# Sparse attention followed by an ELU MoE layer on one Trainium2 core: attention rewritten in residue-class and 96-query blocks, with one table set and a hand-fixed order

## The chip, the cores and the metric

The kernel runs on one core of one Trainium2 chip. The metric is the device time of one execution in microseconds (us), taken over several runs. A ratio is over fast runs alone; it can differ by up to 0.005 from the quotient of the medians that are quoted beside it. Every experiment was timed beside the kernel before on the same chip; experiments of different rounds are therefore compared by their ratios to the kernel before.

The engines are named as in the profile: PE is TensorE's matmuls, PEld its weight loads, ACT is ScalarE, DVE is VectorE, POOL is GpSimd, SP is the queue that stores the output. PSUM is the memory that TensorE's results lie in until another engine has read them. In the chain of waits, "issue" is time in which an engine waited for nothing that the profile shows.

## The reference

Eight batches, eight heads, 576 tokens, head width 64. Heads 0 to 3 look at the last 32 tokens; heads 4 to 7 look at all earlier tokens with the same remainder modulo 32. The attention output is the input of two dense layers with an ELU between them.

```python
scores = q @ k.T / sqrt(64)
rel = pos[:, None] - pos[None, :]
mask_local   = (rel >= 0) & (rel < 32)
mask_strided = (rel >= 0) & (pos[None, :] % 32 == pos[:, None] % 32)
attn = softmax(where(mask, scores, -1e9))        # local for heads 0-3, strided for 4-7
x = (attn @ v)  as [8*576, 512]
h = x @ w_in                                     # 512 -> 2048
g = where(h > 0, h, exp(min(h, 0)) - 1)
out = g @ w_out                                  # 2048 -> 512
```

## The kernel before

Queries and keys are cut into five blocks of 128. A strided head computes every pair of blocks on or below the diagonal and multiplies by a mask; a local head computes the diagonal block and its neighbour. Both heads of a pair are transposed together. The denominators come from a V widened by 64 columns of ones, and are inverted as Exp(-Ln(x)).

```python
for s in range(NQ):                       # blocks of 128 keys
    nq_all = NQ - s if is_str else min(2, NQ - s)
    ...
        nc.tensor.matmul(sc_ps[:, :Nq], lhsT=kT[pb:pb + D, s, :], rhs=qT[...])        # L191
        nc.scalar.activation(exp_sb[:, :Nq], sc_ps[:, :Nq], ACT.Exp, scale=scale)     # L201
        nc.vector.tensor_mul(msk_sb[:, :Nq], exp_sb[:, :Nq], mask_cat[...])           # L207
        nc.tensor.matmul(acc_ps[...], lhsT=v_sb[:, s, p, :], rhs=msk_sb[...])         # L220
nc.scalar.activation(ln_sb[D:2*D, :], acc_ps[D:2*D, ...], ACT.Ln)                     # L235
nc.scalar.activation(recip_sb[D:2*D, :], ln_sb[D:2*D, :], ACT.Exp, scale=-1.0)        # L242
nc.vector.tensor_mul(xT[...], acc_ps[0:D, ...], recip_sb[D:2*D, :S])                  # L247
# after each batch: one chunk of 512 tokens of the MoE
for m in range(16):                       # first layer: 4 matmuls of 512 columns (L269),
    ...                                   # Exp (L276), min/subtract (L279), max (L283)
for kk in range(4):                       # second layer: 16 matmuls (L289), copy (L296), store
    ...
```

The order of each engine's instructions is chosen by the framework's scheduler, which mixes a batch's attention with the MoE of an earlier chunk.

The softmax here doesn't subtract the row's maximum and nothing guards it: scores larger than these inputs give would overflow.

## Time and profile before

| | before |
|---|---|
| median of 4 runs | 684.73 us (678.51 to 685.74) |
| TensorE busy | 503.7 us, 74% |
| ScalarE busy | 480.6 us, 71% |
| MoE matmuls at full pace (estimate: 1152 x 0.216) | 249 us |
| table loads on ScalarE | 129 x 1.283 = 165.5 us |
| mean granted TensorE clock | 0.861 |

The first fence is from the page: busy time, share of the span and instructions of each engine, then the busy tenths in 40 slices for TensorE with the clock granted to it, then the chain of waits by engine.

```profile
PE 503.7 (74%) x2304; PEld 210.1 (31%) x2304; DVE 347.3 (51%) x907; ACT 480.6 (71%) x789; POOL 259.5 (38%) x404
...
PE   0356677779577886989678866878776977679996
...
PEclk9999996899888686569877896589678876999999
...
PE 45%; ACT 28%; issue 17%; DVE 4%; DMA 4%; POOL 1%; ACTq 0%; DVEq 0%; POOLq 0%
```

No engine is full. The clock falls in many slices in the middle, where TensorE's work has gaps.

The groups by form (line, engine, operation, shapes and count, then busy us and mean ns of one, then idle us before it):

```profile
L269 PE MATMUL hps<-xT,w_in_sb 128*128 128x512 bf16 x576 | 199.6, 446 | 9.7 <-DVE xT L247 7.5 <-DVE g_sb L283 1.8
L235 ACT ACT_TABLE_LOAD x64 | 82.1, 1283 | 1.1
L201 ACT ACT_TABLE_LOAD x35 | 44.9, 1283 | 1.4 <-PEq L313 0.8
```

The loads stand before Ln (L235) and before whichever Exp comes next: each switch between the two functions loads a table; 19 and 11 more stand before L242 and L276, 129 in all. In the timeline of ScalarE (start, duration, instruction) the load is wedged between the last score and the logarithm that the denominators wait for, and the next Exp pays again:

```profile
32.11 1.28 ACT L235 ACT_TABLE_LOAD   x1
33.41 0.70 ACT L235 ACTIVATE ln_sb<-acc_ps 64x640 f32<-64x640 f32 x1
34.13 1.28 ACT L201 ACT_TABLE_LOAD   x1
35.42 0.38 ACT L201 ACTIVATE exp_sb<-sc_ps 128x256 bf16<-128x256 f32 x1
```

TensorE waits for ScalarE in the scores, as the waits say (engine and line, whom it waited for, us in total, times, longest):

```profile
PE sc_ps L191 <- ACT exp_sb L201: 115.0, 57, 3.7
PE tp_ps L162 <- DMA qh<-in_q_dram: 26.4, 1, 26.4
```

What a gap costs beyond itself is in the windows (stretch, its length, TensorE busy and matmuls, granted clock, DMA share, GB/s). A sparse stretch is followed by one at half the clock:

```profile
176.00:180.00 4.00, 0.87 (x5) 1.00 0.90 58
180.00:184.00 4.00, 4.00 (x15) 0.59 0.64 40
184.00:188.00 4.00, 1.82 (x8) 0.50 0.00 0
```

The Trainium skill ("TensorE: Matmul & The Clock Gate", Part 1) says that TensorE's clock is halved after about 3.4 us of idleness and restored after about as much work. The pace in this trace fits the two levels: in a dense stretch sixteen MoE matmuls take 3.62 us, (3.62 - 0.38) / 15 = 0.216 us from start to start; at a granted clock of 0.5 four take 1.89 us (at 431.13), (1.89 - 0.63) / 3 = 0.42 us.

### The profile page before, as it was taken

How to read it: one execution, taken by the hardware profiler on the slowest of the kernel's cores; microseconds unless marked ns; L12 is line 12 of the kernel's file. 1: busy time of each engine (PE TensorE's matmuls, PEld its weight loads, DVE VectorE, ACT ScalarE, POOL GpSimd, SP SyncE). 2: the span in 40 equal slices, each digit the busy share in tenths (PEclk: the TensorE clock that was granted, in tenths of full speed). 3: DMA queues.
4: the chain of work that ended last, by engine and by line, in shares of the span. 5: the costliest groups of instructions: out<-in, count | busy, mean ns of one | idle time of the engine just before them, and what ended most of it. 6: DMA issues, size and time to landing. Idle time of an engine off the chain costs nothing.

```text
span 680.3 us, 7667 instructions
## 1 busy us (share of the span) xinstructions
PE 503.7 (74%) x2304; PEld 210.1 (31%) x2304; DVE 347.3 (51%) x907; ACT 480.6 (71%) x789; POOL 259.5 (38%) x404
## 2 busy tenths in 40 slices
PE   0356677779577886989678866878776977679996
PEld 0122232224233332323233322333322433234442
DVE  3144355664456444565556544563555635646570
ACT  0287798974888478784988687884879578974341
POOL 6498456560444415343444433352444410000000
PEclk9999996899888686569877896589678876999999
DMA  8988446461444414345344533344444510001101
GB/s 159 127 57 54 26 27 39 28 39 63 27 27 27 55 38 28 22 25 89 26 28 26 58 48 23 20 31 77 28 26 27 57 39 2 1 16 48 47 15 62
DMA packets 124552, 28.29 MB, mean 42 GB/s; under 512 B 117344, under 2 KB 119392, under 8 KB 124512
## 3 DMA queue, kind: packets, MB, share of 16 engines
q0 software_dynamic: 119328, 18.37, 36.7%
q1 hardware_dynamic: 5184, 9.44, 3.7%
q8 instruction: 18, 0.29, 0.2%
q14 instruction: 22, 0.18, 0.1%
HBM read 36.70 MB, written 9.44 MB: 68 GB/s over the span
## 4 chain that ended last, share of the span: by engine, by line
PE 45%; ACT 28%; issue 17%; DVE 4%; DMA 4%; POOL 1%; ACTq 0%; DVEq 0%; POOLq 0%
PE ops L289 15%; PE hps L269 14%; PE sc_ps L191 8%; ACT exp_sb L201 7%; PE acc_ps L220 6%; ACT ln_sb L235 6%; ACT L235 5%; ACT recip_sb L242 4%; ACT e_sb L276 3%; PE tp_ps L162 3%; DMA kh<-in_k_dram 2%; DVE g_sb L283 2%; DMA w_in_sb<-in_moe_w_in_dram 2%; ACT L276 2%; DVE e_sb L279 1%
## 5 line engine op out<-in xcount | busy, mean ns | idle before, releaser
L269 PE MATMUL hps<-xT,w_in_sb 128*128 128x512 bf16 x576 | 199.6, 446 | 9.7 <-DVE xT L247 7.5
L191 PE MATMUL sc_ps<-qT,kT 64*128 64x256 bf16 (+2 forms) x352 | 98.5, 332 | 120.3 <-ACT exp_sb L201 115.0
L201 ACT ACTIVATE exp_sb<-sc_ps 128x256 bf16<-128x256 f32 (+2 forms) x352 | 129.8, 403 | 67.8 <-PE sc_ps L191 63.0
L289 PE MATMUL ops<-w_out_sb,g_sb 128*128 128x512 bf16 x576 | 158.0, 402 | 10.6 <-ACT o_sb L296 6.4
L143 POOL DMA_DIRECT2D vh<-in_v_dram x64 | 52.5, 820 | 196.0 <-PE acc_ps L220 118.3
L276 ACT ACTIVATE e_sb<-hps 128x512 f32<-128x512 f32 x144 | 84.8, 602 | 26.2 <-PE hps L269 25.4
L283 DVE TENSOR_TENSOR g_sb<-e_sb,hps 128x512 bf16<-128x512 bf16 x144 | 97.4, 682 | 2.0
L269 PEld LDWEIGHTS <-w_in_sb 128*128 128x128 bf16 x576 | 53.9, 106 | 139.8 <-issue 108.0
L207 DVE TENSOR_TENSOR msk_sb<-exp_sb,mask_str 128x512 bf16<-128x512 bf16 (+1 forms) x192 | 56.5, 322 | 74.5 <-ACT exp_sb L201 72.2
L207 DVE TENSOR_TENSOR msk_sb<-exp_sb,mask_local 128x256 bf16<-128x256 bf16 (+1 forms) x160 | 41.1, 277 | 99.9 <-ACT exp_sb L201 97.4
L220 PE MATMUL acc_ps<-msk_sb,vh 128*128 128x128 bf16 (+3 forms) x480 | 90.0, 320 | 0.0
L143 POOL DMA_DIRECT2D qh<-in_q_dram x64 | 53.8, 841 | 90.0 <-PE tp_ps L162 71.2
L296 ACT COPY o_sb<-ops 128x512 f32<-128x512 f32 x36 | 21.1, 587 | 91.2 <-PE ops L289 69.8
L289 PEld LDWEIGHTS <-g_sb 128*128 128x128 bf16 x576 | 56.9, 101 | 89.7 <-issue 27.7
L235 ACT ACT_TABLE_LOAD x64 | 82.1, 1283 | 1.1
L247 DVE TENSOR_TENSOR xT<-acc_ps,recip_sb 64x576 bf16<-64x576 f32 x64 | 48.0, 750 | 65.0 <-ACT recip_sb L242 64.0
L279 DVE TENSOR_SCALAR e_sb<-e_sb 128x512 bf16<-128x512 f32 x144 | 61.6, 443 | 30.9 <-ACT e_sb L276 30.6
L191 PEld LDWEIGHTS <-kT 64*128 64x128 bf16 x352 | 27.3, 99 | 147.6 <-issue 128.5
L220 PEld LDWEIGHTS <-vh 128*128 128x128 bf16 x480 | 50.5, 123 | 39.8 <-issue 25.8
L143 POOL DMA_DIRECT2D kh<-in_k_dram x64 | 56.1, 876 | 3.6 <-DMA w_in_sb<-in_moe_w_in_dram 3.6
L235 ACT ACTIVATE ln_sb<-acc_ps 64x640 f32<-64x640 f32 x64 | 44.8, 699 | 6.9 <-PE acc_ps L220 6.2
L242 ACT ACTIVATE recip_sb<-ln_sb 64x640 bf16<-64x640 f32 x64 | 46.9, 733 | 1.3
(38 smaller groups left out, 347.1 us busy)
## 6 DMA issues: line engine op xcount, KB each, us to landing
out_dram<-o_sb SPq DMA_DIRECT2D x36, 256.0 KB, 2.0
qh<-in_q_dram POOLq DMA_DIRECT2D x64, 64.0 KB, 2.7
kh<-in_k_dram POOLq DMA_DIRECT2D x64, 64.0 KB, 2.7
vh<-in_v_dram POOLq DMA_DIRECT2D x64, 64.0 KB, 2.7
w_in_sb<-in_moe_w_in_dram POOLq DMA_DIRECT2D x1, 2048.0 KB, 12.8
w_out_sb<-in_moe_w_out_dram POOLq DMA_DIRECT2D x1, 2048.0 KB, 19.9
qh<-in_q_dram POOLq DMA_DIRECT2D x64, 8.0 KB, 2.1
kh<-in_k_dram POOLq DMA_DIRECT2D x64, 8.0 KB, 2.2
```

What stands on the lines that cost most here:

```text
L143: nc.gpsimd.dma_start(out=t_sb[:, 0:NQ - 1, hi, :D], in_=src[b, h0 + hi, 0:(NQ - 1) * 128, :].rearrange("(slab p) d -> p slab d", p=128),)
L191: nc.tensor.matmul(sc_ps[:, :Nq], lhsT=kT[pb:pb + D, s, :], rhs=qT[pb:pb + D, s0:s0 + nq, :].rearrange("p a b -> p (a b)"), start=True, st ...
L201: nc.scalar.activation(exp_sb[:, :Nq], sc_ps[:, :Nq], ACT.Exp, scale=scale,)
L207: nc.vector.tensor_mul(msk_sb[:, :Nq], exp_sb[:, :Nq], mask_cat[:, chunk0:chunk0 + nq, :].rearrange("p a b -> p (a b)"),)
L220: nc.tensor.matmul(acc_ps[:, t:t + ntt, :].rearrange("p a b -> p (a b)"), lhsT=v_sb[:, s, p, :], rhs=msk_sb[:, tt * 128:(tt + ntt) * 128], ...
L235: nc.scalar.activation(ln_sb[D:2 * D, :], acc_ps[D:2 * D, :, :].rearrange("p a b -> p (a b)"), ACT.Ln,)
L242: nc.scalar.activation(recip_sb[D:2 * D, :], ln_sb[D:2 * D, :], ACT.Exp, scale=-1.0,)
L269: nc.tensor.matmul(hps, lhsT=w_in_sb[:, c, m * 128:(m + 1) * 128], rhs=xblk[:, c, :], start=(c == 0), stop=(c == KC - 1),)
L276: nc.scalar.activation(e_sb, hps, ACT.Exp)
L279: nc.vector.tensor_scalar(e1_sb, e_sb, scalar1=1.0, scalar2=1.0, op0=ALU.min, op1=ALU.subtract,)
L283: nc.vector.tensor_tensor(g_sb[:, m, :], e1_sb, hps, op=ALU.max)
L289: nc.tensor.matmul(ops, lhsT=g_sb[:, m, kk * 128:(kk + 1) * 128], rhs=w_out_sb[:, m, :], start=(m == 0), stop=(m == MC - 1),)
```

## The change

Its intent is to make attention small and to hide it under the MoE. Strided heads are split by the remainder of the token modulo 8: each class has 72 tokens, so a head needs eight blocks of 72 x 72 in place of fifteen of 128 x 128. Local heads use six blocks of 96 queries against 128 keys. Exp and Ln share one table set. The load order puts batch 0's attention ahead of the weights. The instruction order is fixed by hand: one piece of the next batch's attention, four first-layer matmuls, four second-layer matmuls, and so on.

```diff
+    ctx.enter_context(tc.manual_schedule())
+    nc.scalar.preload_act_table_set("natural_log_exp_and_others")
+    p_a = ...("ps_a", bufs=2, PSUM)      # transposes, outputs and sums share this
...
+    def load_str(src, b, name):          # strided heads: runs of 8 tokens, one DMA for 4 heads
+        nc.gpsimd.dma_start(out=t, in_=src[b, HG:2*HG].rearrange("h (p s) d -> p h (s d)", s=NS))
...
+    def piece_T(P):                      # transpose q, then k; one shared buffer each
+        ...  nc.tensor.transpose(ps[:, o:o+RS], src[...], identity[...])
+             nc.vector.tensor_copy(dst, ps)
+    def piece_S(P, u):                   # half of a pair: scores of both halves of the array, Exp, mask
+        nc.tensor.matmul(sc[:, z, i*n:(i+1)*n], lhsT=P.kT[pr, k0:k0+128], rhs=P.qT[pr, o:o+n], ...)
+        nc.scalar.activation(e[0:R], sc[0:R, :, 0:W], ACT.Exp, scale=scale)
+    def piece_O(P, u, pm):               # o_ps and s_ps: both shared buffers
+        ...
+        nc.scalar.activation(ln, s_ps, ACT.Ln)
+        nc.scalar.activation(rc, ln, ACT.Exp, scale=-1.0)
+        if P.str:
+            dst = xs.rearrange("c (p u sp z) -> c u z sp p", u=2, sp=2, z=2)[:, u]
+            nc.vector.tensor_mul(dst, o_ps.rearrange(pat, ...), rc.rearrange(pat, ...))   # L275
+        else:
+            nc.vector.tensor_mul(xs[:, u*W:(u+1)*W], o_ps, rc)                            # L278
...
+    def run_piece(p):
+        old = list(pend); pend.clear()
+        if u < 0: piece_T(...)
+        else:     pend.append(... piece_S(...))
+        for a in old: piece_O(*a)
...
+    for nb in range(NCH):
+        for m in range(MC):
+            run_piece(pieces[done])      # while there are any
+            l1(nb, m)                    # 4 matmuls, Exp, 2 VectorE operations
+            if nb > 0: l2(nb - 1, m)     # 4 matmuls
```

A pair of heads is three pieces: T (transposes), then the two halves. In the order, the outputs of an older half come behind the new piece: T is followed by the outputs of the previous pair's second half, and the second half by those of the first. There are 96 pieces: 14 run alone, 82 are interleaved, and 62 MoE steps are left.

## The prediction

> **What bounds the kernel now.** The span is 680 us and no engine is full: the busy table gives TensorE 504 us (74%), ScalarE 481 (71%), VectorE 347, GpSimd 260. The chain of waits is shared: TensorE 45%, ScalarE 28%, "issue" 17%. TensorE and ScalarE hold each other up in attention. The groups by form show why ScalarE is long: 129 table loads of 1283 ns (165 us) because Ln and Exp use different tables; 352 score exponentials (138 us); Ln and Exp of the denominators over 64x640 (92 us); the MoE needs only 106 us. TensorE's needed work is less than its busy time: in a dense stretch of the timeline, 16 MoE matmuls take 3.62 us, 0.216 us each start to start, so 1152 of them are 249 us. The windows show a granted clock of 1.0 when TensorE is dense (600-680 us), and 0.5 for several us after sparse stretches (184-188, 220-224 us); mean 0.861. At the start the first transpose waits 26.4 us, because both weights are queued ahead of q.
>
> **What changes, costed.**
> - ScalarE: one table set for Ln and Exp. The Trainium skill ("ScalarE: Activation LUTs", Table sets: the hidden batching unit) says one set holds both and gives 1283 ns a load; the trace agrees on the load. -165 us. By the trace's 0.83 ns per element plus about 0.17 us, each of 64 half-pairs costs 0.65 (Exp 576) + 0.41 + 0.41 (Ln, Exp 288) us: 94 us in place of 230. ScalarE falls to about 200 us.
> - VectorE: two copies at 0.45, two mask products at 0.45 and two normalisations at 0.45 us a pair: 87 us, plus 159 of MoE: about 246 us.
> - TensorE: 1472 small matmuls (448 transposes, 448 scores, 576 values and sums) in place of 1152. The trace's dense 128-column transposes start 0.057 us apart; at 0.06 us, 46 a pair are 2.8 us. Seven changes of tile shape a pair cost about 0.1 us each (the timeline shows that much beyond the streaming time; the skill's "TensorEngine Tiling", Key Properties, says that a change of mode drains the array). Tiny matmuls add about 110 us to 249: TensorE about 360 us, now the bound.
> - DMA: strided heads load in 1 KB runs; packets fall from 119 thousand to about 70 thousand. Not the bound, except at the start.
>
> **Critical path, in four parts.**
> 1. Batch 0's attention plus two pieces, alone: about 13 us until q, k and the identity are there, then 14 pieces at 2.6 us, latency-bound because transposes, outputs and sums share two PSUM buffers: about 50 us.
> 2. 82 interleaved steps. A pair's three steps: 3 x 1.73 (eight MoE matmuls) + 2.8 + 0.7 + about 0.9 of waiting in the transpose step for VectorE to empty those two buffers = 9.5 us, 3.2 a step: 262 us, less 14 for chunk 0, which has no second layer.
> 3. 62 steps of MoE alone at 1.73: 107 us.
> 4. Last second layer 14 us, copy and store 3 us; some clock dips, 8 us.
>
> Sum: 430 us; range 398 to 480. Ratio about 0.63.
>
> **Right if:** at most two table loads; TensorE above 85% busy with the clock near 1.0 after 60 us; ScalarE about 30% of the chain or less; first MoE matmul at 45-60 us; attention ends near 300 us; last 62 steps at 1.73 us.
>
> **Wrong if:** table loads remain (about 550 us); small matmuls cost 0.1 us or more, since 64-column weight loads and shape changes do not overlap (+50 us); in-order queues make TensorE wait each step for ScalarE or VectorE, and the clock drops to half again (+50 us or more); or batch 0's local heads, still in 128-byte packets, come late.
>
> Chances: faster by over 2% 0.98, within 2% 0.01, slower 0.01.

## The result, and the profile after

The kernel after takes 423.29 us (median of 4 runs, 420.37 to 423.34) against 684.73: the ratio is 0.6187, 95% interval 0.6153 to 0.6222. The same parts of the page, after:

```profile
PE 345.6 (82%) x2584; PEld 171.2 (41%) x2624; DVE 271.7 (64%) x501; ACT 196.7 (47%) x373; POOL 88.9 (21%) x120
...
PE   0256776678888878888887888888999999999996
...
PEclk9999988989988998998999889899999999999999
...
PE 61%; DVE 15%; DMA 9%; ACT 6%; issue 4%; POOL 4%; POOLq 0%; ACTq 0%
```

ScalarE has left the chain (28% to 6%); TensorE and VectorE hold it. The groups:

```profile
L318 PE MATMUL hps<-xT,w_in_sb 128*128 128x512 bf16 x542 | 152.4, 403 | 5.5 <-issue 5.2
...
L275 DVE TENSOR_TENSOR xT<-o_ps,rc 128x288 bf16<-128x288 f32 x32 | 46.0, 1437 | 20.0 <-ACT rc L269 20.0
...
L278 DVE TENSOR_TENSOR xT<-o_ps,rc 128x288 bf16<-128x288 f32 x32 | 14.6, 458 | 19.0 <-ACT rc L269 19.0
...
L61 ACT ACT_TABLE_LOAD x1 | 1.3, 1283 | 0.8 <-PEq L388 0.8
```

One table load is left. The two normalisations have the same size, 288 elements on 128 partitions, but the strided heads' one (L275) takes three times the other's time.

The stages, from the first and last instructions in the timeline, beside those of the prediction:

| stage | predicted us | measured us |
|---|---|---|
| batch 0 and two pieces, until the first MoE matmul's weights are loaded | 50 | 43.9 |
| 82 interleaved steps | 262 - 14 = 248 | 252.4 (43.9 to 296.3) |
| 62 steps of MoE alone | 107 | 106.4 (1.72 each) |
| last second layer, copy, store | 17, and 8 for the clock anywhere | 18.9 |

The windows of the last two stages (columns: stretch, length, busy us and count of PE, PEld, DVE, ACT and POOL, granted clock, DMA share, GB/s) show where the kernel is good and where not:

```profile
96.00:296.00 200.00, 169.94 (x1470) 84.47 (x1491) 144.22 (x261) 107.09 (x211) 38.77 (x49) 0.94 0.47 56
296.00:403.00 107.00, 106.37 (x493) 48.54 (x502) 69.64 (x126) 46.22 (x79) 0.00 (x0) 1.00 0.10 38
```

In the interleaved stage TensorE stands still 15% of the time and does not have its full clock. Why is in its timeline, over one pair of strided heads (in brackets the idle time before an instruction, and what ended it):

```profile
151.03 0.30 PE L217 MATMUL sc<-qT_130,kT_127 64*128 64x72 bf16 x8
151.27 1.04 PE L318 MATMUL hps<-xT,w_in_sb 128*128 128x512 bf16 x4
...
155.45 0.42 PE L185 MATMUL tp<-identity,qs 72*128 72x72 bf16 x8
156.62 0.42 PE L185 MATMUL tp<-identity,ks 72*128 72x72 bf16 x8 [0.76 <-DVE xT L275]
157.97 0.45 PE L240 MATMUL s_ps<-pm,ones 72*64 72x288 bf16 x2 [0.92 <-DVE qT_131 L196]
...
159.11 1.49 PE L318 MATMUL hps<-xT,w_in_sb 128*128 128x512 bf16 x3 [0.33 <-issue]
```

The two half pieces take 2.07 and 2.35 us with their eight MoE matmuls. The T piece, from 155.45 to the next scores at 161.85, takes 6.40. It is one of the longest: from 85 us on the T pieces take 3.98 to 6.67 us, 4.96 on average (22 of them), and the long ones are those that run into half clock. The clock record has 11 stretches at half clock between 59 and 274 us, of 3.41 us each. The transposes of k need the buffer that the previous outputs still hold, and wait for their normalisation; the sums need the buffer of q, and wait for its copy; then the MoE matmuls behind them start 0.43 us apart in place of 0.216 - half the clock. VectorE's timeline of the same stretch shows what was in front of that copy: the slow strided normalisation and the two ELU operations of the previous step.

```profile
155.14 1.44 DVE L275 TENSOR_TENSOR xT<-o_ps,rc 128x288 bf16<-128x288 f32 x1 [0.32 <-ACT rc L269]
156.20 0.62 DVE L325 TENSOR_SCALAR he_1943<-he 128x512 bf16<-128x512 f32 x1
156.86 0.69 DVE L327 TENSOR_TENSOR g<-he_1943,hps 128x512 bf16<-128x512 bf16 x1
157.46 0.45 DVE L196 COPY qT_131<-tp 128x576 bf16<-128x576 bf16 x1
```

So the total was predicted to 2%, but the middle stage holds a stall that is larger than the one predicted, and something else must be smaller. The experiments take this apart, and measure what the table set, the interleaving and the fixed order are worth. No run changes the block sizes or the load order alone.

### The profile page after: what moved, and what is told of

Its sections match the earlier page's. It is cut to its first block, busy times and chain, and to the rows that moved or that the text cites. A ratio compares the mean times of both kernels' runs of the same rounds, so it can differ in the third digit from the quotient of the medians.

```text
span 421.6 us, 6645 instructions
## 1 busy us (share of the span) xinstructions
PE 345.6 (82%) x2584; PEld 171.2 (41%) x2624; DVE 271.7 (64%) x501; ACT 196.7 (47%) x373; POOL 88.9 (21%) x120
## 4 chain that ended last, share of the span: by engine, by line
PE 61%; DVE 15%; DMA 9%; ACT 6%; issue 4%; POOL 4%; POOLq 0%; ACTq 0%
PE hps L318 28%; PE ops L339 27%; DVE xT L275 4%; DVE g L327 4%; DMA ks<-in_k_dram 3%; DMA qs<-in_q_dram 3%; PE sc L217 3%; ACT he L323 2%; DMA vs<-in_v_dram 2%; PE o_ps L261 1%; ACT e L221 1%; ACT rc L269 1%; PE o_ps L249 1%; PE s_ps L256 1%; ACT osb L344 1%
## 5 line engine op out<-in xcount | busy, mean ns | idle before, releaser
L318 PE MATMUL hps<-xT,w_in_sb 128*128 128x512 bf16 x542 | 152.4, 403 | 5.5 <-issue 5.2
L339 PE MATMUL ops<-w_out_sb,g 128*128 128x512 bf16 x570 | 151.0, 392 | 0.4
L323 ACT ACTIVATE he<-hps 128x512 f32<-128x512 f32 x144 | 85.8, 596 | 87.3 <-PE hps L318 84.4
L339 PEld LDWEIGHTS <-g 128*128 128x128 bf16 x576 | 58.0, 101 | 72.6 <-issue 8.2
L221 ACT ACTIVATE e<-sc 72x576 bf16<-72x576 f32 (+1 forms) x64 | 41.4, 648 | 42.6 <-PE sc L217 41.3
L275 DVE TENSOR_TENSOR xT<-o_ps,rc 128x288 bf16<-128x288 f32 x32 | 46.0, 1437 | 20.0 <-ACT rc L269 20.0
L267 ACT ACTIVATE ln<-s_ps 128x288 f32<-128x288 f32 x64 | 26.1, 407 | 68.9 <-PE s_ps L240 39.1
L75 POOL DMA_DIRECT2D ql<-in_q_dram x32 | 23.6, 747 | 38.4 <-PE tp L192 27.2
L269 ACT ACTIVATE rc<-ln 128x288 f32<-128x288 f32 x64 | 28.3, 443 | 2.0
L75 POOL DMA_DIRECT2D kl<-in_k_dram x32 | 23.8, 755 | 16.5 <-DMA qs<-in_q_dram 6.2
L278 DVE TENSOR_TENSOR xT<-o_ps,rc 128x288 bf16<-128x288 f32 x32 | 14.6, 458 | 19.0 <-ACT rc L269 19.0
L185 PE MATMUL tp<-identity,qs 72*128 72x72 bf16 x128 | 7.7, 210 | 14.5 <-POOL identity L112 13.9
```

The source lines that it names most:

```text
L75: nc.gpsimd.dma_start(out=t[:, h // 2, :, h % 2, :], in_=src[b, h].rearrange("(t p) d -> p t d", p=LQ))
L185: nc.tensor.transpose(ps[:, o:o + RS], src[:, P.g0 + x, 2 * sp * D:2 * (sp + 1) * D], identity[0:RS, 0:RS])
L221: nc.scalar.activation(e[0:R], sc[0:R, :, 0:W], ACT.Exp, scale=scale)
L267: nc.scalar.activation(ln, s_ps, ACT.Ln)
L269: nc.scalar.activation(rc, ln, ACT.Exp, scale=-1.0)
L275: nc.vector.tensor_mul(dst, o_ps.rearrange(pat, z=2, sp=2), rc.rearrange(pat, z=2, sp=2))
```

## The experiments

Twelve kernels ran. Ratios are to the kernel before; the change itself has 0.6187.

### One table set in the kernel before, nothing else

```diff
     nc = tc.nc
+    nc.scalar.preload_act_table_set("natural_log_exp_and_others")
```

> The kernel before plus one line that makes the table set holding both Exp and Ln active at the start; nothing else of the change. Both theories expect 1 table load in place of 129 and ScalarE's busy time down by about 165 us, to about 315 us. Theory (engines hold each other up, the loads lie only partly on the chain of waits, about a tenth of the span): the span falls by 50 to 100 us, to 585 to 635 us, and the rest of the gain of the change comes from other parts. Rival (the gain of the change is mostly the removal of table loads): the span falls by 150 us or more, to 535 us or less.

Measured: 504.92 us (499.64 to 510.16), ratio 0.7365 (0.7274 to 0.7457). One of the four runs was slow and is not in the ratio. The theory fell, and the rival stood: the span of the profiled runs fell from 680.3 to 502.0, by 178 us, which is more than the 165 us that ScalarE was freed of.

```profile
PE 429.1 (85%) x2261; PEld 187.7 (37%) x2304; DVE 346.0 (69%) x907; ACT 314.4 (63%) x661; POOL 260.8 (52%) x404
...
PE   0067878899989998999899988998999889999985
...
PEclk9999999999999999999999999998899999999999
```

The lines say where the rest came from. TensorE's busy time fell from 503.7 to 429.1 us although its matmuls are the same (the profile records a few fewer), and the mean clock rose from 0.861 to 0.992: the first-layer matmul went from 446 to 389 ns in the groups. The scheduler's order did not change with the line: ScalarE's 660 and VectorE's 907 instructions, the loads left out, stand in the same order in both traces. The loads had made the gaps that halved the clock. How much of the 178 us is the loads themselves and how much the clock was not tried apart; the 75 us by which TensorE's busy time fell are an estimate of the clock's part. To take the loads for "about a tenth of the span" from the chain was a wrong way to read it: the chain names the releaser of each step, and a matmul at half pace, or one that waits for the next one, appears there as TensorE.

### The change without the shared table set

```diff
-    nc.scalar.preload_act_table_set("natural_log_exp_and_others")
```

> The kernel after without the line that makes the common table set active; nothing else. About 128 table loads of 1.28 us come back, ScalarE rises from 197 to about 360 us. Theory (TensorE bound, ScalarE has room of about 1 us a step): in the interleaved part ScalarE then needs about 10.4 us a pair against TensorE's 9.2, so 30 to 70 us more, 455 to 495 us. Rival (in-order queues put every load on the chain): all 164 us come back, about 580 us.

Measured: 550.1 us (548.0 to 550.79), ratio 0.805 (0.7985 to 0.8115). Neither: of the 164 us of loads, 127 us came back, between the theory's 30 to 70 and the rival's whole. The groups and the waits:

```profile
L266 ACT ACT_TABLE_LOAD x64 | 82.1, 1283 | 1.1
L268 ACT ACT_TABLE_LOAD x64 | 82.1, 1283 | 1.1
```

```profile
DVE xT L274 <- ACT rc L268: 84.2, 32, 3.0
DVE xT L277 <- ACT rc L268: 84.0, 32, 3.0
...
PE tp L184 <- DVE xT L274: 22.0, 8, 2.8
PE tp L191 <- DVE xT L274: 21.6, 8, 2.8
```

(The line numbers are one lower than after's, since a line is gone.) ScalarE is busy for 66% of the span only, so its throughput is not the limit. The two loads stand between sums and normalisation, so the normalisation waits 2.6 us each time ((84.2 + 84.0) / 64; 0.6 in the run after, (20.0 + 19.0) / 64), the two shared buffers are held longer, TensorE waits for them, and the mean clock falls to 0.835 (TensorE is busy for 396.0 us in place of 345.6 with the same matmuls). A latency inside a chain through two buffers cost more than the count of busy time allowed for.

The prediction had put this case at about 550 us under "wrong if", without a sum behind it; that the figure was met shows nothing of the mechanism.

### All attention first, then all MoE

```diff
-    for _ in range(AHEAD):
+    while done < len(pieces):            # and the loads of batches 2 to 7 as before
         run_piece(pieces[done]); done += 1
+    flush()
     for nb in range(NCH):                # no piece is left for these steps
         for m in range(MC):
             ...
```

> The kernel after with the attention of all 8 batches first and all MoE layers behind it; same instructions otherwise. Theory: attention alone runs at the speed of batch 0, about 1.9 us a piece (14 pieces in 26 us), so 18 + 96 x 1.9 = 200 us, then MoE alone 1152 x 0.216 = 249 us: about 450 us, so interleaving is worth only 25 to 45 us and the rest of the gain of the change is that attention itself became short. Rival (interleaving is the main gain): 500 us or more.

Measured: 470.6 us (470.29 to 471.0), ratio 0.6894 (0.6841 to 0.6948); between the two. Attention ends at 205.7 us, as the theory's sum had it (200); the MoE behind it takes 263 us, not 249, mainly because in chunk 0 the first layer runs alone and waits for VectorE (its 64 matmuls take 24.5 us, and 13.8 at full pace). Interleaving in the fixed order is thus worth 47 us. Part of that is the clock: in attention alone TensorE has the half pace, eight scores take 0.42 us (at 183.12) in place of 0.30. Two lines give a caution about the clock. The first is of the windows of PE, just behind the end of attention; the second is the timeline there:

```profile
206.00:212.00 6.00, 5.08 (x15) 1.00 0.02 4
```

```profile
206.11 3.19 PE L318 MATMUL hps<-xT,w_in_sb 128*128 128x512 bf16 x7 [0.33 <-issue]
```

The granted clock reads 1.00, but seven matmuls in 3.19 us with a last one of 0.63 are 0.43 us apart, half pace. In the run after, too, the record says 1.00 up to 44 us, and the first three MoE matmuls (at 44.31) take 1.49 us, again 0.43 us apart. So in these traces a mean clock is an upper bound. The Trainium skill ("TensorE: Matmul & The Clock Gate", Part 1) warns that these records have been unreliable; this trace agrees.

### The change in the scheduler's order

```diff
-    ctx.enter_context(tc.manual_schedule())
```

> The kernel after with the fixed order taken away: the framework's own scheduler orders the instructions of each engine from the same program. Theory (work per engine decides, the order matters little as long as both kinds of work are mixed): within 5% of the kernel after, 400 to 445 us. Rival (the order is a main part of the gain, since the scheduler's order left TensorE waiting in the kernel before): 460 us or more.

Measured: 379.61 us (378.96 to 381.4), ratio 0.5569 (0.5523 to 0.5614). Both sides of the expectation fell: the order matters, and the fixed one is the worse, by 11% (0.6187 / 0.5569). The work is the same, down to the strided normalisation at 1436 ns. The granted clock of the profiled run is 1.0, and TensorE is busy for 140 of 150 us between 100 and 250. Around a T piece the scheduler did this: transposes of q and k at 156.32 and 156.57, four first-layer matmuls at 156.84, the sums at 157.85, one second-layer matmul, the outputs at 158.42. MoE matmuls fill the time that VectorE needs to copy q and k.

```profile
156.57 0.43 PE L184 MATMUL tp<-identity,ks 72*128 72x72 bf16 x8
156.84 1.03 PE L317 MATMUL hps<-xT,w_in_sb 128*128 128x512 bf16 x4
```

### The fixed order with that one place mended

In the step with T, the old outputs are emitted behind the first-layer matmuls:

```diff
-            run_piece(pieces[done]);  l1(nb, m)            # T, old outputs, first layer, second layer
+            late = run_piece(pieces[done], defer=True)     # T leaves its old outputs for later
+            l1(nb, m)
+            for a in late: piece_O(*a)
```

> The kernel after with one change of its fixed order: in the step that transposes, the sums and outputs of the old half-pair are emitted behind the four first-layer matmuls instead of ahead of them. Theory (the fixed order loses because TensorE stands in that step for VectorE to empty the two shared buffers, about 25 us in the waits of the sums for the copies of q, and because the clock is then halved for some us, a mean of about 0.93 in the interleaved part): the waits of the sums for the copies nearly vanish, the mean clock rises to 0.98 or more, and the time falls to 378 to 395 us, close to the scheduler's 380. Rival (the scheduler gains by mixing everywhere, or by starting MoE earlier, not by this one place): 405 us or more.

Measured: 385.92 us (383.93 to 387.8), ratio 0.5653 (0.5613 to 0.5693), as the theory expected. This edit alone gives 0.0534 of the 0.0618 by which the scheduler's order is ahead. In the timeline of TensorE the same place is now without a wait:

```profile
155.31 0.42 PE L192 MATMUL tp<-identity,ql 96*128 96x96 bf16 x6
155.56 0.42 PE L192 MATMUL tp<-identity,kl 96*128 96x96 bf16 x6
155.82 1.03 PE L321 MATMUL hps<-xT,w_in_sb 128*128 128x512 bf16 x4
156.84 0.31 PE L256 MATMUL s_ps<-pm,ones 128*64 128x288 bf16 x2
```

In the waits, the sums' wait for the copy of q, 25 us over the run after, is down to 1.1 us, and the clock from 100 to 250 us, where both runs interleave, is 1.00 in place of 0.93. What is left is the wait of the transposes of k for the strided normalisation, 11.5 us.

### The strided write made contiguous (wrong result)

```diff
-            dst = xs.rearrange("c (p u sp z) -> c u z sp p", u=2, sp=2, z=2)[:, u]
+            dst = xs[:, u * W:(u + 1) * W].rearrange("c (z sp p) -> c z sp p", z=2, sp=2)
```

> The kernel after with the strided heads' normalised outputs written to consecutive columns instead of every eighth pair of bytes (wrong result on purpose: tokens stand in another order). Theory (the slow strided write, 1437 against 458 ns, lies on the chain, since the transposes of k and the copies wait behind it): the write takes about 0.46 us, VectorE's busy time falls by 31 us, the time by 12 to 30 us, to 393 to 411 us. Rival (VectorE has slack, the wait is for the buffers anyway): within 2% of 423 us.

Measured: 398.23 us (396.26 to 401.57), ratio 0.5836 (0.5788 to 0.5884); the tokens are out of order, as intended. The theory held. Only the destination differs, and the instruction takes 457 ns in place of 1437:

```profile
L275 DVE TENSOR_TENSOR xT<-o_ps,rc 128x288 bf16<-128x288 f32 x32 | 14.6, 457 | 19.4 <-ACT rc L269 19.4
```

So the write, not the four-dimensional pattern of its reads, made it slow: (1437 - 457) / 288 = 3.4 ns more for each element. The Trainium skill ("SBUF — State Buffer", Door 1: The DMA port swizzle) says that SBUF has lines of 16 bytes and that each access which crosses into a new line pays; the destination's neighbours stand 16 bytes apart, so each write meets a new line. That agrees; the page gives no size for it.

### The same write in runs of four elements (correct result)

```diff
-            dst = xs.rearrange("c (p u sp z) -> c u z sp p", u=2, sp=2, z=2)[:, u]
-            pat = "c (z sp p) -> c z sp p"
+            dst = xs.rearrange("c (p u sp z) -> c u p sp z", u=2, sp=2, z=2)[:, u]
+            pat = "c (z sp p) -> c p sp z"
```

> The kernel after with the strided heads' normalisation walked in token order: four consecutive elements are written before the step of 16 bytes, and the reads of PSUM and of the reciprocals are strided instead; correct result. Theory (each separate two-byte write at a stride costs): the instruction falls from 1437 ns to between 450 and 800 ns and the time comes near that of the contiguous write. Rival (the 4-dimensional pattern or the reads cost, or the bytes of a line are written one by one anyway): it stays at 1.4 us, and so does the time.

Measured: 399.98 us (398.61 to 401.78), ratio 0.586 (0.5822 to 0.5898): the time of the contiguous write within the intervals, and with the right result.

```profile
L275 DVE TENSOR_TENSOR xT<-o_ps,rc 128x288 bf16<-128x288 f32 x32 | 20.5, 640 | 19.3 <-ACT rc L269 19.3
```

Walking the same elements in the order of the destination, with the stride moved to the reads, took the instruction from 1437 to 640 ns. Whether the 183 ns that are left over the contiguous write lie in the writes or in the strided reads was not tried apart.

### Three shared buffers

```diff
-    p_a = ...(name="ps_a", bufs=2, ...)      p_o = ...(name="ps_o", bufs=2, ...)
+    p_a = ...(name="ps_a", bufs=3, ...)      p_o = ...(name="ps_o", bufs=1, ...)
```

> The kernel after with three instead of two PSUM buffers for transposes, outputs and sums, and one instead of two for the second layer. Theory (TensorE waits in the transposing step for those buffers to be emptied): the waits of the transposes of k for the normalisation and half of the waits of the sums for the copy of q go, the time falls by 10 to 35 us, less about 3 us at the end for the single second-layer buffer: 390 to 413 us. Rival (the wait is for VectorE's queue, not for a buffer): within 2% of 423 us.

Measured: 390.06 us (388.64 to 392.29), ratio 0.5717 (0.5678 to 0.5756), the theory's lower end. The wait of the transposes of k for the normalisation is gone from the waits; 8.9 us of waiting for it have moved to the sums. A slow writer, a bad order and a missing buffer are three ways into the same stall: each mend alone gives 23 to 37 us, 94 in all, while the three together, with the earlier start below, give 58.

### Score matmuls issued twice

On the kernel with the deferred outputs:

```diff
-        for i in range(4 if P.str else 3):
+        for i in list(range(4 if P.str else 3)) * 2:
```

> The kernel with the deferred outputs, every score matmul issued twice (448 more small matmuls, the same result). It measures the term that the prediction put at 0.06 us each. By the prediction's figure: 27 us more than 386. By the starts in the trace, where eight score matmuls take 0.23 us to the next instruction, 0.03 us each: 10 to 15 us more, 396 to 401 us.

Measured: 391.84 us (391.06 to 393.52), ratio 0.5748 (0.5716 to 0.5779), against 0.5653 without. The difference of 0.0095 is 6.5 us of 682, for 448 matmuls 14 ns each; with intervals of 0.004 and 0.003 it is a rough figure, 3 to 10 us, but it rules out the 27 us of the prediction's 0.06 us each, and misses the 10 to 15 us expected here as well. The timeline after agrees: eight scores span 0.30 us of which the last takes 0.20, so 14 ns from start to start. The scores go to the two halves of the array in turn, and the Trainium skill ("TensorE: Matmul & The Clock Gate", Part 3) says that matmuls in different tiles of the array run at the same time. The trace agrees: at the MoE's 0.216 us for 512 columns, 72 columns one after the other would be 30 ns (an estimate), twice the 14 ns. The 0.23 us to the next instruction, from which 0.03 was read, contains the change of the array's shape, paid once for the group.

### Versions that beat both

`auto_early` is the scheduler's order with the identity and the masks built ahead of the loads on GpSimd's queue: in the kernel after, the first transpose waited 13.9 us for the identity, though q was there at 6.5. `auto_all` adds the four-element write and the three buffers. `defer_all` is the same in the fixed order with the deferred outputs.

```diff
+    identity = ...; ones = ...; mask_s = ...; mask_l = ...      # moved up
     batch_in[0] = load_batch(0)
```

> The kernel after without the fixed order and with the identity and masks built ahead of the loads. Theory (the first transpose waited 13.9 us for the identity while q was there at 6.5 us): it starts at about 7 us and the time is 5 to 9 us below the 380 of the scheduler's order: 371 to 375 us. Rival (what follows waits for the weights or for the local heads anyway): 377 us or more.

> A version meant to beat both: the kernel after without the fixed order, with the four-element walk of the strided normalisation, three shared PSUM buffers and one for the second layer, and the identity and masks built ahead of the loads on the load queue. Theory (each mends a different wait: the slow write, the buffers, the 7 us between the arrival of q and the identity): 350 to 370 us. Rival (the scheduler's order has already hidden the write and the buffers, only the start is left): 370 to 380 us.

> The same three mends with the fixed order kept and the deferred outputs of the run before: theory: 355 to 372 us, so that a fixed order is no worse than the scheduler's once its one bad place is mended. Rival (the scheduler's order is better by itself): at least 8 us above the other combined version.

Measured: `auto_early` 374.99 us (374.3 to 375.41), ratio 0.5499 (0.5467 to 0.5532). `auto_all` 366.54 us (363.92 to 369.85), ratio 0.5361 (0.5324 to 0.5397). `defer_all` 365.1 us (364.29 to 366.91), ratio 0.5356 (0.5326 to 0.5386). All three are in the ranges of their theories. The last two are equal: a fixed order is no worse than the scheduler's once its one bad place is mended, and the rival there falls. One pair in the timeline of TensorE of `defer_all`, from its first scores to the next pair's, takes 157.89 - 150.43 = 7.46 us:

```profile
150.43 0.30 PE L217 MATMUL sc<-qT,kT 64*128 64x72 bf16 x8
...
152.50 0.30 PE L217 MATMUL sc<-qT,kT 64*128 64x72 bf16 x8
...
154.85 0.42 PE L185 MATMUL tp<-identity,qs 72*128 72x72 bf16 x8
...
157.89 0.30 PE L217 MATMUL sc<-qT,kT 64*128 64x72 bf16 x7
```

This is what the three steps cost next to without a stall, and it gives the terms of the prediction: 7.46 less 3 x 1.73 of MoE leaves 2.3 us for all small matmuls and changes of shape of this pair. Over 19 pairs, strided and local, from one transposition of q at 89.3 us to that at 227.8, the mean is 7.29 us, which leaves 2.1.

## Why the prediction was right or wrong

The predicted 430 us and the measured 423 differ by 2%, and each of the four stages is within some us of its forecast. The largest stage was right through two errors that cancel, which is luck.

- **What bounds the kernel before.** Right that TensorE and ScalarE hold each other up and that the loads are 165 us of ScalarE. The prediction did not say what the loads are worth in time; the expectation of the first experiment did, at 50 to 100 us, and was wrong: 178 us.
- **One table load.** Right: 1 in place of 129. This one line, put into the kernel before, brings the ratio to 0.7365; the whole change has 0.6187. The rest of the change takes the time from 505 to 423 us, and without its fixed order to 380.
- **ScalarE about 200 us; its share of the chain 30% or less.** Right: 196.7 us, 6%.
- **VectorE about 246 us.** Short by 26 us: 271.7. The term that was mis-sized is "two normalisations at 0.45 us a pair". For strided pairs each took 1.437 us, 32 x 0.98 = 31 us more, because the write with a stride of 16 bytes had been costed like the contiguous one.
- **Small matmuls 2.8 us and seven changes of shape 0.7 us a pair.** Too large. The pairs of `defer_all` show 2.1 us on average for both together, and the doubled scores about 14 ns for each score in place of 60. The pace had been taken from full-width transposes, one after the other. Over the 82 / 3 = 27.3 pairs of the stage, (3.5 - 2.1) x 27.3 = 38 us were predicted and not spent (an estimate from these means).
- **About 0.9 us of waiting in the T step.** The place was right and the size was not. From one transposition of q at 88.3 us to that at 287.9, 21 pairs of the kernel after take 9.50 us each, as predicted, where `defer_all` needs 7.29: 2.2 us are lost, with the half clock that follows, in place of 0.9 ((2.2 - 0.9) x 27.3 = 35 us more over the stage, by the same estimate). So the two errors nearly cancel. The deferred outputs and the third buffer show that the wait is there, and that the slow write makes it longer; it was not foreseen that MoE matmuls put between T and the outputs remove it.
- **TensorE over 85% busy and the clock near 1.0 after 60 us.** Missed: 82%, and a clock of 0.93 between 44 and 296 us (the same between 100 and 250). With the one place mended it is 87%, and 1.00 between 100 and 250 us.
- **First MoE matmul at 45 to 60 us, attention ends near 300, the last steps at 1.73.** 44.3 (its weights at 43.9), 296.3 and 1.72: the first just outside its range, on the early side. "About 13 us until q, k and the identity are there" was right (13.9), and avoidable; the 14 pieces behind it took (43.9 - 13.9) / 14 = 2.1 us each in place of 2.6.
- **From 119 to about 70 thousand packets.** The load queue, for which the 119 stand, has 76.3 thousand (81.5 with all queues); in the run after no matmul waits for a DMA in the list of waits.

What stays open: how the 178 us of the table loads divide into the loads and the half clock that followed them; and why taking them out of the kernel before gains 176 us but putting them back into the kernel after costs 127. The orders and the number of buffers differ between the two, and no run separates them. Open too is how the step from 505 us (the kernel before with one table set) to 380 (the kernel after in the scheduler's order) divides between the smaller blocks, the fewer and wider instructions and the load order.

## What to carry to other kernels

Count the table loads first: two functions that alternate in a chain between TensorE's matmuls cost more than their busy time, since the gaps that they open also halve TensorE's clock, and one line that makes a common table set active may remove them. When an order is fixed by hand, look at each place where TensorE's next instruction needs a buffer that another engine must empty, and put independent matmuls there; compare with the scheduler's order before keeping the hand-made one. A prediction that adds up can hide two wrong terms, so check each term against the trace, not only the sum.

## What the Trainium skill lacked or had wrong

- "ScalarE: Activation LUTs", Table sets: the hidden batching unit, says that Ln followed by Exp needs one load. That is true of the set, not of what one gets: without the line that makes the set active, the runs show 129 loads (before) and 129 (the change without the line).
- The same page, What ACT_TABLE_LOAD costs, adds a drain of about 1380 ns to each load of 1283 ns (it is this section, not the one that the prediction names, that has the 1283). The load agrees to the ns, but no drain is seen on either side: in the timeline before, the last score's Exp starts at 31.71 and takes 0.38 us, the load starts at 32.11 and the logarithm behind it at 33.41.
- "SBUF — State Buffer" tells of the 16-byte lines without a size for VectorE, and "VectorE: DVE Perf Modes" (Mode 1×) says of the mode that takes fp32 and PSUM operands, as here, only that it works with odd strides too. Measured: 1437 ns for 288 elements 16 bytes apart, 640 in runs of four, 457 contiguous.
- "TensorE: Matmul & The Clock Gate", Back-to-back issue gap, gives about 131 ns a matmul at 512 columns in a stream with weight loads, and about 216 for a single one. Sixteen in 3.62 us, each with its own weights, are 216 ns each here, and the 62 steps of MoE alone take 1.72 us for eight, 215 each.
- "TensorEngine Tiling", Key Properties, says that a change of mode drains the array and gives no time; eight scores of 14 ns and the step to the next shape take 0.23 us together, which leaves about 0.1 us for the change (an estimate from these two).
